# Attention products as pairs of 64-column tiles, one run per head, with new engine orders

## The chip, the cores and the metric

The kernel runs on one core of a Trainium2 chip, in one launch. The metric is the device time of that core in microseconds (us), the median of several runs. One execution was also recorded by the hardware profiler; its rows are what the working below rests on. Engine names are those of the profile: PE (TensorE, matrix products; PEld its weight loads), DVE (VectorE), ACT (ScalarE), POOL (GpSimd), SP (the queue that issues nearly all DMAs).

## The reference

Causal attention over 8 batches of 12 heads, 448 positions and 64 dimensions a head, followed by a soft mixture of experts on the result (3584 tokens of width 768, 8 experts of 4 slots):

```python
scores = scale * np.matmul(q, k.transpose(0, 1, 3, 2))
scores = np.where(mask, -1000000000.0, scores)          # mask: key behind query
scores = scores - np.max(scores, axis=-1, keepdims=True)
attn = np.exp(scores)
attn = attn / (np.sum(attn, axis=-1, keepdims=True) + 1e-09)
x = np.matmul(attn, v)                                  # then heads side by side: (3584, 768)

logits = x @ phi                                        # phi: (768, 32 slots)
slot_input = softmax_over_tokens(logits).T @ x
h = np.maximum(slot_input[e] @ w1[e], 0.0)              # per expert e, 4 slots each
slot_out[e] = h @ w2[e]
out = softmax_over_slots(logits) @ slot_out
```

All of it is float32 in and out.

## The kernel before

**Stages.** A short start (casts and the first scores), then a loop over the 96 heads (`for i in range(NHD)`), then the experts and the output. The loop works on pairs of heads (p = i // 2, h = i % 2), since q and k come in as pairs. While it runs, DMAs also bring the first 23 pieces of expert weights; the rest of the weights comes in after the loop.

**A head's way through the loop** is spread over several iterations. In iteration i:

- `scores1(i+2, ...)` on PE: the causal mask (parts c3, c0, c12, a product of `identb` and `tri`) and the first part of the scores (k0 to k3) go into a PSUM tile `s`, of which there are three. A head's scores are 4 blocks of 128 keys against the queries that may see them, 1024 columns in all.
- `max_keys(i+2, 0..3)` on DVE (x0 to x3): x0 is one TRANSPOSE_TENSOR_REDUCE of `s` (PSUM) into `r` (SBUF), x1 to x3 are three small TENSOR_TENSOR maxima of `r` with `r`, both inputs in SBUF.
- `max_row(i+1, 0)` (mr0): PE transposes `r` into the PSUM tile `rt`. `max_row(i+1, 1)` (mr1): DVE reduces `rt` to `mr`.
- `max_spread(i+1)` (sp): POOL spreads `mr` with an AFFINE_SELECT into rows of `r2` (the profile prints its name as `r`).
- `scores2(i, ...)` (t0 to t3) on PE: adds the rest of the scores and the spread maximum to `s`.
- `exps(i)` (exp): ACT writes exp(s) into `pt`, a tile in SBUF with one buffer for even and one for odd heads.
- `attv(i-1, ...)` (a0 to a3): PE multiplies blocks of `pt` with `va` (values and a column of ones, 65 columns) into the one PSUM tile `po`. Query block qc needs qc + 1 products, so 10 a head. Each is float32 and runs as two passes of one weight load and one matmul; the profile counts passes.
- `norm(i-1, 0..2)` (n0 to n2): DVE makes `sm` from `po` (a TENSOR_SCALAR and a RECIPROCAL) and writes `x` = `po` times `sm`.
- For the pair after next: `cast_k`, `cast_q` (ck, cq) and `copy_k2` (c2) on ACT; `sub_k` (sk, in even iterations) and `sub_q` (sq, in odd ones) on POOL, one TENSOR_TENSOR each, of two SBUF inputs.
- `plan`: in iterations fixed by number, one piece of the mixture: `xtrans` (4 transposes of `x` into `xt`, copied by ACT to `xts`), `next_logits` (8 products into `g` in tiles of 32 columns, then DVE adds into `lt`), `logits_e` (2 transposes into `tp`), `dispatch` (4 products into `sp` in tiles of 32 columns, then a DVE accumulation into `si`). `rt`, `xt`, `g`, `tp` and `sp` share one PSUM buffer (tag "m"), so the next one waits until the one before has been read.

**Order.** Nothing is reordered: every engine runs its instructions in the order in which the code emits them, and the framework adds the semaphore waits. Within an iteration that order is written out by hand, in the table `ORDER`, one row for even and one for odd iterations; an entry adds its instructions to the end of its own engine's queue. So the order on DVE is the order of the x, mr1 and n entries among each other, that on POOL the order of sp with sk or sq, and so on. "ld" runs a piece of the logits on ACT in one iteration of 12.

Of the kernel before, what the change touches and what calls it, by code (L numbers as in the profile page):

```python
# [17 lines left out]
P = 128  # L18
NB, NH, S, HD = 8, 12, 448, 64
NPAIR = NB * NH // 2  # L20
PPB = NH // 2
DM = NH * HD
NT = NB * S
NSLOT, NEXP, FF = 32, 8, 1024
# [6 lines left out]
NHD = 2 * NPAIR  # L31
# [13 lines left out]


ORDER = (
# [4 lines left out]
)  # L52

SC0, SC1, SC2, SC3 = 512, 0, 320, 960
# [30 lines left out]
def attention_soft_moe(ctx: ExitStack, tc: tile.TileContext, qk, va, phi, w1, w2, out):  # L85
    nc = _Core(tc)
# [36 lines left out]
    st = {}  # L123
# [199 lines left out]
        if i < NHD:  # L323
            nc.scalar.activation(out=pt_[i % 2][:, 0:1024], in_=st.pop(("s", i)), func=AF.Exp, scale=SCALE)

    def attv(i, qcs, first):
        if not 0 <= i < NHD:
            return
        p, h = divmod(i, 2)
        pt, v, po = pt_[i % 2], va_[p % 2], st.get(("po", i), po0)  # L330
        for qc in qcs:
            for c in range(qc + 1):
                col = SCOL[c] + P * (qc - c)


                m = P if qc < 3 or i == NHD - 1 and c < 3 else 65
                nc.tensor.matmul(po[0:m, qc], pt[:, col:col + m], v[:, c, h],
                                 start=c == 0 and qc in first, stop=c == qc, skip_group_check=True)

    def norm(i, k):  # L340
        if not 0 <= i < NHD:
# [20 lines left out]
    def xtrans(p):  # L362
        x = st.pop(("x", p))
        pt = misc(f"xt{p}")
        for c in range(NCH):
            nc.tensor.transpose(out=pt[:, P * c:P * c + P], in_=x[:, c], identity=ident)
        xt = st["xt", p] = xtp.tile([P, 512], F32, tag="xt", name=f"xts{p}", bufs=2)
        nc.scalar.activation(out=xt, in_=pt, func=AF.Copy)

    def logits_a(b, js, g, first=True, last=True):  # L370

        for j in js:
            xt = st.pop(("xt", b * PPB + j))
            for c in range(NCH):
# [14 lines left out]
    def logits_d(b, l):  # L389
        mo, mn = run_m[(b + 1) % 2], run_m[b % 2]  # L390
        al = st["al", b] = moe.tile([P, 1], F32, tag="al", name=f"al{b}", bufs=2)
        bs = st["bs", b] = moe.tile([P, 1], F32, tag="bs", name=f"bs{b}", bufs=2)
        nc.scalar.activation(out=gs, in_=l, func=AF.Exp, bias=mn[:, 0:1], accum_out=bs)
        nc.scalar.activation(out=al, in_=mo, func=AF.Exp, scale=-1.0, bias=mn[:, 0:1])
# [5 lines left out]
    def logits_e(b):  # L400
        tp = misc(f"tp{b}")
        nc.tensor.transpose(out=tp[:, 0:P], in_=gs, identity=ident)
        nc.tensor.transpose(out=tp[:, P:2 * P], in_=lt, identity=ident)
        st["dn", b] = gs.rearrange("p (c s) -> p c s", s=NSLOT)
        nc.scalar.activation(out=gs, in_=tp[:, 0:P], func=AF.Copy)
        nc.scalar.activation(out=lg[:, b], in_=tp[:, P:2 * P], func=AF.Copy)
        nc.scalar.activation(out=run_z, in_=run_z, func=AF.Identity, scale=st["al", b][:, 0:1],
                             bias=st.pop(("bs", b))[:, 0:1])
# [21 lines left out]
        dispatch_a(b, hf, sp)  # L430
        dispatch_b(b, hf, sp)

    plan = {}
    for b in range(NB):
        o, last = 12 * b, b == NB - 1
        for j, r in enumerate((3, 5, 9, 10, 12, 13)):
            if not last or j < PPB - 2:
                plan[o + r] = lambda p=b * PPB + j: xtrans(p)
        for j, r in ((0, 8), (2, 11)):
            plan[o + r] = lambda b=b, j=j: next_logits(b, j, misc(f"g{b}_{j}"))  # L440
        if not last:
            plan[o + 14] = lambda b=b: (next_logits(b, 4, misc(f"g{b}_4")), logits_b(b, lt))
            plan[o + 16] = lambda b=b: logits_e(b)
            plan[o + 18] = lambda b=b: dispatch(b, 0)
            plan[o + 19] = lambda b=b: dispatch(b, 1)

# [43 lines left out]
    run_z = const.tile([P, 1], F32, name="run_z")  # L490
    si = const.tile([P, DM], F32, tag="si", name="si")
    lg = const.tile([P, NB, NCH, NSLOT], F32, name="lg")
# [17 lines left out]
    for i in range(NHD):  # L510
        p, h = divmod(i, 2)
        if h:
            load_qk(p + 3, 1)
            if p + 1 < NPAIR - 1:
                loads_v(p + 1)
            load_qk(p + 3, 0)
            if p % 2 and nload < RES:
                load_w(nload)
                nload += 1
        if i == NHD - 3:  # L520

            loads_v(NPAIR - 1, nc.scalar)
        if i < 2:
            scores2(i, (1, 0, 2))
            if i:
                scores1_all(3)
            scores2(i, (3,))
            exps(i)
            if i == 0:
                max_row(1, 0)  # L530
                warm(START[4], po0.rearrange("p a b->p (a b)")[:, 0:P])
                max_row(1, 1)
                sub_k(1, h1, nc.vector)
                max_spread(1)
                sub_q(1, h1)

        qs = [int(n[1]) for n in ORDER[h] if n[0] == "a"]
        first = qs[:2] if qs[0] == 3 else qs[:1]
        for n in ORDER[h]:
            if i < 2 and (n == "exp" or n[0] in "kt" or n in ("c0", "c3", "c12")):  # L540
                continue
            if i == 0 and n in ("mr0", "mr1", "sp"):
                continue
            if n[0] == "k" or n in ("c0", "c3", "c12"):
                scores1(i + 2, n)
            elif n[0] == "t":
                scores2(i, (int(n[1]),))
            elif n[0] == "a":
                attv(i - 1, (int(n[1]),), first)
            elif n[0] == "x":  # L550
                max_keys(i + 2, int(n[1]))
            elif n[0] == "n":
                norm(i - 1, int(n[1]))
            elif n in ("mr0", "mr1"):
                max_row(i + 1, int(n[2]))
            elif n == "ld":
                if i % 12 == 3 and i > 12:
                    logits_d(i // 12 - 1, lt)
            elif n == "plan":
                if later and i:  # L560
                    later.pop(0)()
                plan.get(i, int)()
            else:
                {"exp": lambda: exps(i), "sp": lambda: max_spread(i + 1),
                 "ck": lambda: cast_k(p + 2), "sk": lambda: sub_k(p + 2), "cq": lambda: cast_q(p + 2),
                 "c2": lambda: copy_k2(p + 1), "sq": lambda: sub_q(p + 2)}[n]()
        if i == NHD - 1:

            scs.close()
            pe = att.enter_context(tc.tile_pool(name="pe", bufs=1, space=PSUM, reuse_waits="tile"))  # L570
            ps = [pe.tile([P, 512], F32, name=f"e{k}") for k in range(6)]

    i, b, p = NHD - 1, NB - 1, NPAIR - 1
# [8 lines left out]

    for k, qcs in ((2, (3, 2)), (4, (1, 0))):
        po = st["po", i] = ps[k][:, 0:NCH * VC].rearrange("p (c n) -> p c n", n=VC)
        attv(i, qcs, qcs[:1])
        cs = slice(qcs[1], qcs[0] + 1)
        nc.vector.tensor_scalar(out=sm[:, cs], in0=po[:, cs, HD], scalar1=EPS, scalar2=None, op0=ALU.add)
        nc.vector.reciprocal(out=sm[:, cs], in_=sm[:, cs])
        nc.vector.tensor_tensor(out=x[:, cs, HD:2 * HD], in0=po[:, cs, 0:HD],
                                in1=sm[:, cs].unsqueeze(2).to_broadcast([P, 2, HD]), op=ALU.mult)  # L590
# [17 lines left out]
    for c in range(NCH):  # L608
        nc.tensor.matmul(lp[32 * c:32 * c + 32, 0:P], phis[1][:, 2], xa[:, P * c:P * c + P],
                         start=False, stop=True, skip_group_check=True)  # L610
# [16 lines left out]
    for c in range(NCH):  # L627
        nc.tensor.matmul(tm[32 * c:32 * c + 32, P:P + 1], nm[:, 0:NSLOT], ident[:, 0:1],
                         start=True, stop=True, skip_group_check=True)
# [12 lines left out]
    for hf in range(2):  # L642
        tps = po0.rearrange("p a b->p (a b)")[:, 0:96] if hf == 0 else ps[2][:, 0:96]
        for c in range(3):
            o = 384 * hf + P * c
            nc.tensor.matmul(tps[:, NSLOT * c:NSLOT * c + NSLOT], si[:, o:o + P], sidw,
                             start=True, stop=True)
# [20 lines left out]

    hsb = const.tile([P, DM], F32, tag="si", name="hsb")

    def expert_in(e):
        hp = pt2.tile([P, 512], F32, tag="h", name=f"hp{e}")
        for dc in range(PPB):
            for f in range(4):
                k = 4 * dc + f
                w = wtiles[0, e, k // 12, k // 6 % 2][:, 256 * (k % 6):256 * (k % 6) + 256]
                nc.tensor.matmul(hp[32 * f:32 * f + 32, 0:256], slt[dc // 3][:, dc % 3], w,
                                 start=dc == 0, stop=dc == PPB - 1, skip_group_check=True)
        if e == 0:
# [119 lines left out]
    n = NBUF  # L799
# [42 lines left out]
def _layout(q, k, v, moe_phi, moe_w1, moe_w2):  # L842
# [9 lines left out]
    va = vp.reshape(NPAIR, 2, NCH, P, VC).transpose(0, 3, 2, 1, 4)  # L852
    phi = moe_phi.reshape(PPB, P, NSLOT).transpose(1, 0, 2)
    w1 = moe_w1.reshape(NEXP, PPB, P, 4, 256).transpose(0, 2, 1, 3, 4)
# [28 lines left out]
```

## Time and profile before

| what | value |
|---|---|
| median of 3 runs | 467.58 us (467.29 to 470.31) |
| the profiled execution: its own time | 467.8 us |
| its span, first to last instruction | 466.0 us, 1.8 us less than its time |
| mean granted TensorE clock | 0.985 |
| busy, of the span | PE 429.8, PEld 368.3, DVE 338.5, ACT 288.5, POOL 266.7 us |
| HBM read, written | 107.25 MB, 11.01 MB |

A row of the time view reads: start in us, duration in us, engine, line, operation, output <- inputs, shapes, count, and in brackets the idle time before it with what ended it. Several instructions of one kind in succession are merged into one row, whose duration is from the first start to the last end. All instructions of the kernel carry the line of the helper that records them, so groups are told apart by their tiles.

### The profile page before, as it was taken

The page shows a single profiled execution, that of the slowest core. Times are in us where ns is not written, and L with a number is a line of the kernel's source. Part 1 is how long each engine was busy: PE and PEld are TensorE (multiplying, and loading weights), DVE is VectorE, ACT ScalarE, POOL GpSimd, SP SyncE. Part 2 cuts the span into 40 slices and gives each one's busy share as a digit, 9 for nine tenths or more (in the row PEclk, how much of TensorE's full clock was granted, in tenths as well). Part 3 has the DMA queues.
Part 4 walks back from the last instruction along what each step waited for, and adds up shares of the span by engine and source line. Part 5 has one row for each costly group of instructions (what it writes and reads, how often), then busy time and mean ns, then how long its engine had stood idle before and what let it go on. Part 6 is the DMA issues. An engine that isn't in the chain of part 4 may idle for free.

```text
span 466.0 us, 11818 instructions
## 1 busy us (share of the span) xinstructions
PE 429.8 (92%) x4628; PEld 368.3 (79%) x4628; DVE 338.5 (73%) x954; ACT 288.5 (62%) x400; POOL 266.7 (57%) x216
## 2 busy tenths in 40 slices
PE   7799999999999999999999999999999999899850
PEld 3688998898999899988998899889988864454430
DVE  6888788878787888788788877887888447634350
ACT  5576777577767777777677677767774411243240
POOL 5788777776777677767776777677765100000000
PEclk9999999999999999999999999999999999999995
DMA  7376666765676656755676656765667999999998
GB/s 265 105 244 218 201 220 210 234 210 183 207 244 234 208 181 211 239 207 190 213 245 224 201 184 219 229 227 184 232 210 243 403 367 426 423 422 413 404 391 346
DMA packets 34471, 119.02 MB, mean 255 GB/s; under 512 B 3824, under 2 KB 8944, under 8 KB 32880
## 3 DMA queue, kind: packets, MB, share of 16 engines
q1 hardware_dynamic: 34272, 118.01, 71.8%
q8 instruction: 36, 0.59, 0.5%
q10 hardware_dynamic: 144, 0.27, 0.2%
q14 instruction: 19, 0.16, 0.1%
HBM read 107.25 MB, written 11.01 MB: 254 GB/s over the span
## 4 chain that ended last, share of the span: by engine, by line
PE 69%; DVE 14%; DMA 12%; issue 1%; ACT 1%; SPq 0%
PE po L69 31%; PE s L69 21%; DMA w<-in_w_dram 11%; DVE r L69 7%; PE xt L69 5%; PE sp L69 2%; DVE run_m L69 2%; PE g L69 2%; PE rt L69 2%; PE pp L69 1%; PE e L69 1%; DVE x L69 1%; DVE sm L69 1%; PE hp L69 1%; DMA qk<-in_qk_dram 1%
## 5 line engine op out<-in xcount | busy, mean ns | idle before, releaser
L69 PE MATMUL po<-va,pt 128*128 128x65 f32 x1900 | 193.3, 250 | 0.2 <-ACT xts L69 0.2
L69 PEld LDWEIGHTS po<-va,pt 128*128 128x128 f32 x1900 | 190.6, 170 | 0.5 <-ACT xts L69 0.4
L69 ACT ACTIVATE pt<-s 128x1024 f32<-128x1024 f32 x96 | 98.4, 1025 | 87.0 <-PE s L69 84.5
L69 DVE TRANSPOSE_TENSOR_REDUCE r<-s 128x32 f32<-128x1024 f32 x96 | 119.9, 1249 | 26.5 <-PE s L69 23.9
L69 POOL TENSOR_SCALAR_AFFINE_SELECT r<-mr 14x448 fp32r<-14x448 f32 x96 | 62.1, 646 | 86.9 <-DVE mr L69 60.4
L69 POOL TENSOR_TENSOR r<-qk,qd 64x896 fp32r<-64x896 f32 (+1 forms) x50 | 101.4, 2027 | 6.6 <-ACT qd L69 2.8
L69 POOL TENSOR_TENSOR ks<-qk,ks 64x896 fp32r<-64x896 f32 (+1 forms) x47 | 97.7, 2080 | 3.7
L69 PE MATMUL s<-r,k 128*128 128x320 f32 (+3 forms) x384 | 82.9, 297 | 2.2 <-POOL r L69 2.1
L69 PE MATMUL s<-qd,ks 128*128 128x448 f32 (+3 forms) x384 | 76.0, 308 | 0.9 <-ACT qd L69 0.8
L69 DVE TENSOR_TENSOR r<-r 128x10 f32<-128x10 f32 (+2 forms) x288 | 58.7, 204 | 9.8
L69 PEld LDWEIGHTS s<-r,k 128*128 128x128 f32 (+1 forms) x384 | 59.9, 176 | 5.8 <-POOL r L69 3.5
L69 PEld LDWEIGHTS s<-qd,ks 128*128 128x128 f32 (+1 forms) x384 | 55.1, 181 | 2.4 <-ACT qd L69 1.8
L69 ACT ACTIVATE ks<-qk 128x896 fp32r<-128x896 f32 (+1 forms) x50 | 45.7, 916 | 3.9 <-DMA qk<-in_qk_dram 2.7
L69 ACT ACTIVATE k<-ks 64x896 fp32r<-64x896 f32 (+1 forms) x49 | 45.8, 935 | 1.2
L69 ACT ACTIVATE qd<-qk 128x896 fp32r<-128x896 f32 (+1 forms) x50 | 45.7, 913 | 0.4 <-DMA qk<-in_qk_dram 0.3
L69 DVE TENSOR_TENSOR x<-po,sm 128x256 f32<-128x256 f32 x95 | 40.3, 425 | 3.3
L69 PEld LDWEIGHTS <-identb 128*128 128x128 bf16 x339 | 29.2, 99 | 16.5 <-issue 14.7
L69 PE MATMUL s<-tri,identb 128*128 128x64 bf16 (+2 forms) x288 | 39.8, 235 | 0.0
L69 PE MATMUL xt<-ident,x 128*128 128x128 f32 x188 | 29.9, 282 | 7.7 <-DVE mr L69 7.4
L69 ACT ACTIVATE xts<-xt 128x512 f32<-128x512 f32 x47 | 28.1, 597 | 11.5 <-PE xt L69 9.7
L69 DVE TENSOR_SCALAR sm<-po 128x4 f32<-128x4 f32 x95 | 15.1, 159 | 23.1 <-PE po L69 22.7
L69 DVE TENSOR_REDUCE mr<-rt 14x32 f32<-14x128 f32 x96 | 26.7, 278 | 2.5 <-PE rt L69 2.2
(135 smaller groups left out, 365.9 us busy)
## 6 DMA issues: line engine op xcount, KB each, us to landing
qk<-in_qk_dram SPq DMA_DIRECT2D x94, 448.0 KB, 3.3
w<-in_w_dram SPq DMA_DIRECT2D x43, 768.0 KB, 6.3
w<-in_w_dram SPq DMA_DIRECT2D x10, 1536.0 KB, 18.9
va<-in_va_dram SPq DMA_DIRECT2D x47, 260.0 KB, 3.4
out_dram<-ot SPq DMA_DIRECT2D x16, 384.0 KB, 6.7
out_dram<-ot SPq DMA_DIRECT2D x2, 1536.0 KB, 9.2
qk<-in_qk_dram SPq DMA_DIRECT2D x4, 224.0 KB, 3.4
hw<-in_w_dram SPq DMA_DIRECT2D x1, 768.0 KB, 6.3
```

The costliest lines, as they stand in the source:

```text
L69: return self._tc.keep_in_program_order(op(*args, **kwargs))
```

## The change

`attv` issues its products on 64 columns of `pt` at a time, instead of 128 (or 65 for the last query block): the output goes to partitions 0 to 63 or 64 to 127 of `po`, so that for query blocks 0 to 2 two products lie side by side in the array. The last query block (64 queries) is one product of 64 columns per key block. That is 16 products a head for 10. A set in `st` keeps which half of the tile has begun, for the start flag.

`ORDER` is rewritten. The 16 products of a head stand in one run at the end of an iteration, behind the scores, the transposed maximum and the transposes of `xtrans`; before, the products of query blocks 0 and 3 stood around the last part of the scores (t3), those of 1 and 2 behind it. `xtrans` and `logits_e`, whose matmuls are full width, move out of `plan` into an own table `plan_a`, called ahead of the run ("pa"); `next_logits` and `dispatch`, with their 32-column tiles, stay behind it. mr0, mr1 and sp now stand right behind the first part of the scores, ahead of t0 to t3 and of x0 to x3. On POOL the order stays sp, then sk or sq.

```diff
+AW = 64
 ORDER = (
-    ("c3", "c0", "k3", "c12", "k1", "k0", "k2", "t0", "t2", "t1", "a0", "a3", "t3", "ck",
-     "mr0", "exp", "x0", "a2", "x1", "x2", "x3", "mr1", "a1", "cq", "sp", "n0", "sk", "n1", "ld", "n2", "plan"),
-    ("c3", "c0", "k3", "c12", "k0", "k1", "k2", "t0", "t1", "t2", "a0", "x0", "t3", "a3", "exp", "mr0",
-     "x1", "x2", "x3", "mr1", "sp", "a2", "a1", "n0", "ld", "n1", "n2", "sq", "c2", "plan"),
+    ("ck", "c3", "c0", "k3", "c12", "k1", "k0", "k2", "mr0", "mr1", "sp", "sk", "t0", "t2", "t1", "t3", "exp", "pa",
+     "x0", "x1", "x2", "x3", "cq", "a0", "a1", "a2", "a3", "n0", "n1", "n2", "ld", "plan"),
+    ("c3", "c0", "k3", "c12", "k0", "k1", "k2", "mr0", "mr1", "sp", "t0", "t1", "t2", "t3", "sq", "exp", "c2", "pa",
+     "x0", "x1", "x2", "x3", "a0", "a1", "a2", "a3", "n0", "n1", "n2", "ld", "plan"),
 )
...
-    def attv(i, qcs, first):
+    def attv(i, qcs):
...
+        begun = st.setdefault(("begun", i, id(po)), set())
         for qc in qcs:
             for c in range(qc + 1):
                 col = SCOL[c] + P * (qc - c)
-                m = P if qc < 3 or i == NHD - 1 and c < 3 else 65
-                nc.tensor.matmul(po[0:m, qc], pt[:, col:col + m], v[:, c, h],
-                                 start=c == 0 and qc in first, stop=c == qc, skip_group_check=True)
+                for u in range(0, P if qc < 3 or i == NHD - 1 and c < 3 else 64, AW):
+                    nc.tensor.matmul(po[u:u + AW, qc], pt[:, col + u:col + u + AW], v[:, c, h],
+                                     start=u not in begun, stop=c == qc, skip_group_check=True)
+                    begun.add(u)
...
-    plan = {}
+    plan, plan_a = {}, {}
...
-                plan[o + r] = lambda p=b * PPB + j: xtrans(p)
+                plan_a[o + r] = lambda p=b * PPB + j: xtrans(p)
...
-            plan[o + 16] = lambda b=b: logits_e(b)
+            plan_a[o + 16] = lambda b=b: logits_e(b)
...
+            elif n == "pa":
+                plan_a.get(i, int)()
```

DVE's queue over one iteration, in the kernel before, in the middle of the loop: `s` and `r` are the scores and maxima of head i + 2, `rt` and `mr` those of head i + 1, `sm` and `x` the norm of head i - 1.

```order
L69 TENSOR_REDUCE r_2084<-s_2072 128x32
L69 TENSOR_TENSOR r_2084<-r_2084 128x10
L69 TENSOR_TENSOR r_2084<-r_2084 128x6
L69 TENSOR_TENSOR r_2084<-r_2084 128x2
L69 TENSOR_REDUCE mr_2097<-rt_2092 14x32
L69 TENSOR_SCALAR sm_2105<-po 128x4
L69 RECIPROCAL sm_2105<-sm_2105 128x4
L69 TENSOR_TENSOR x_100<-po,sm_2105 128x4x64
```

And DVE's queue in the changed kernel, over one iteration at the same head:

```order
L70 TENSOR_REDUCE mr_2298<-rt_2296 14x32
L70 TENSOR_REDUCE r_2315<-s_2288 128x32
L70 TENSOR_TENSOR r_2315<-r_2315 128x10
L70 TENSOR_TENSOR r_2315<-r_2315 128x6
L70 TENSOR_TENSOR r_2315<-r_2315 128x2
L70 TENSOR_SCALAR sm_2336<-po 128x4
L70 RECIPROCAL sm_2336<-sm_2336 128x4
L70 TENSOR_TENSOR x_100<-po,sm_2336 128x4x64
L70 TENSOR_REDUCE mr_2351<-rt_2349 14x32
```

Read as a circle, the eight instructions are the same, but `mr` has moved: before it stood between the three maxima and the norm, now it stands behind the norm and ahead of the next TRANSPOSE_TENSOR_REDUCE. POOL's rows beside it, in the changed kernel (in the kernel before they stand in the same order):

```order
L70 AFFINE_SELECT r_94<-mr_2298 14x448
L70 TENSOR_TENSOR r_91<-qk_20_2171,qd_85 64x896
L70 AFFINE_SELECT r_94<-mr_2351 14x448
L70 TENSOR_TENSOR ks_90<-qk_21_2283,ks_90 64x896
```

The spread of each `mr` is followed at once by one subtraction; nothing moved here, and each spread waits for the DVE row that writes its `mr`.

PE's queue from the transposed maximum to the next head's first scores, in the kernel before:

```order
L69 MATMUL s_1971<-r_91,k_93 128x448
L69 MATMUL s_1971<-r_91,k_93 128x320
L69 MATMUL s_1971<-r_91,k_93 128x192
L69 MATMUL po<-va_92,pt_95 128x65
L69 MATMUL s_1971<-r_91,k_93 64x64
L69 MATMUL po<-va_92,pt_95 65x65 x4
L69 MATMUL rt_2092<-ident,r_2041 14x128
L69 MATMUL po<-va_92,pt_95 128x65 x5
L69 MATMUL xt_2111<-ident,x_99 128x128 x4
```

And in the changed kernel:

```order
L70 MATMUL rt_2296<-ident,r_2257 14x128
L70 MATMUL s_2175<-r_91,k_93 128x448
L70 MATMUL s_2175<-r_91,k_93 128x320
L70 MATMUL s_2175<-r_91,k_93 128x192
L70 MATMUL s_2175<-r_91,k_93 64x64
L70 MATMUL xt_2308<-ident,x_99 128x128 x4
L70 MATMUL po<-va_92,pt_95 64x65 x16
```

The transposed maximum moved ahead of the second part of the scores, the products of `po` became one run of 16 behind everything else of the head, and the transposes of `x` stand ahead of that run instead of behind it.

More of the change, by code (lines that the diff above doesn't have):

```diff
@@ L535, in attention_soft_moe @@
                 sub_q(1, h1)
-        qs = [int(n[1]) for n in ORDER[h] if n[0] == "a"]
-        first = qs[:2] if qs[0] == 3 else qs[:1]
         for n in ORDER[h]:
@@ L548, in attention_soft_moe @@
             elif n[0] == "a":
-                attv(i - 1, (int(n[1]),), first)
+                attv(i - 1, (int(n[1]),))
             elif n[0] == "x":
@@ L584, in attention_soft_moe @@
         po = st["po", i] = ps[k][:, 0:NCH * VC].rearrange("p (c n) -> p c n", n=VC)
-        attv(i, qcs, qcs[:1])
+        attv(i, qcs)
         cs = slice(qcs[1], qcs[0] + 1)
```

## The prediction

> **What bounds the kernel now.** I first cut the span where the head loop ends, and read the busy time of each engine in the two stretches.
>
> ```profile
> core 0: us, PE busy (x) PEld busy (x) DVE busy (x) ACT busy (x) POOL busy (x), PEclk, DMA share, GB/s
> 18.06:363.80 345.74, 335.98 (x3628) 313.44 (x3629) 280.98 (x794) 248.80 (x315) 253.67 (x196) 1.00 0.65 213
> 364.00:466.00 102.00, 80.19 (x909) 46.23 (x907) 45.12 (x137) 28.13 (x69) 0.84 (x2) 0.93 1.00 401
> ```
>
> The second stretch, the experts, moves data with its DMA share at 1.00; the change touches nothing in it, and what it does to the loop only shifts it. In the loop PE is busy 97% of the time, DVE 81%, POOL 73%, DMA 65%, and the granted clock (PEclk) is full. So the loop decides. The length of a head comes from an instruction that runs once in 12 heads, in seven of the eight batches, with its first and last start:
>
> ```profile
> L69 DVE TENSOR_TENSOR run_m<-run_m,bm x7: 1284/1285/1303, 68.2 to 336.5; 128x1 f32<-128x1 f32 x7
> ```
>
> (336.5 - 68.2) / 72 heads = 3.73 us a head. Next I read what one head costs PE, from the chain of waits in order of time (start, us, engine and what):
>
> ```profile
> 194.52 1.14 PE s L69 x10
> 195.66 0.19 PE po L69 x2
> 195.85 0.03 PE s L69
> 195.88 0.50 PE po L69 x8
> 196.38 0.11 PE rt L69
> 196.49 1.06 PE po L69 x10
> 197.56 0.48 PE xt L69 x4
> ```
>
> The sum is 3.51 us, of which 1.75 are the 20 passes of `po`. Every head has one such extra as `xt` at the end. A reader who stops here would take all that is saved on `po` off the time. So I also read how DVE and POOL wait for each other (start, us, engine, operation):
>
> ```profile
> 208.96 0.28 DVE L69 TENSOR_REDUCE mr<-rt 14x32 f32<-14x128 f32 x1
> 209.31 0.64 POOL L69 TENSOR_SCALAR_AFFINE_SELECT r<-mr 14x448 fp32r<-14x448 f32 x1 [0.69 <-DVE mr L69]
> 209.49 0.16 DVE L69 TENSOR_SCALAR sm<-po 128x4 f32<-128x4 f32 x1 [0.25 <-PE po L69]
> 209.68 0.18 DVE L69 RECIPROCAL sm<-sm 128x4 f32<-128x4 f32 x1
> 209.90 0.42 DVE L69 TENSOR_TENSOR x<-po,sm 128x256 f32<-128x256 f32 x1
> 210.03 2.10 POOL L69 TENSOR_TENSOR ks<-qk,ks 64x896 fp32r<-64x896 f32 x1
> 210.46 1.25 DVE L69 TRANSPOSE_TENSOR_REDUCE r<-s 128x32 f32<-128x1024 f32 x1
> 211.74 0.81 DVE L69 TENSOR_TENSOR r<-r 128x10 f32<-128x10 f32 x3
> 212.47 0.28 DVE L69 TENSOR_REDUCE mr<-rt 14x32 f32<-14x128 f32 x1
> 212.82 0.64 POOL L69 TENSOR_SCALAR_AFFINE_SELECT r<-mr 14x448 fp32r<-14x448 f32 x1 [0.69 <-PE po L69]
> ```
>
> The reader is to see two things. POOL starts its subtraction (2.10 us) as soon as the spread is done. And the three maxima of `r` take 0.81 us here, from 211.74, though they come one right behind the other: the first is still running when the subtraction ends at 212.13. Such a **hold** is plainest where a DVE instruction of 128x1 with both inputs in SBUF meets a subtraction:
>
> ```profile
> 201.64 2.10 POOL L69 TENSOR_TENSOR ks<-qk,ks 64x896 fp32r<-64x896 f32 x1
> 202.47 1.28 DVE L69 TENSOR_TENSOR run_m<-run_m,bm 128x1 f32<-128x1 f32 x1
> ```
>
> One element a partition takes 1.28 us, and ends at 203.75, 0.01 behind POOL's 203.74. All seven of its kind do so (1284 to 1303 ns, quoted above). Instructions with PSUM among their inputs, and the reciprocal of one input, run beside POOL without such a stretch: RECIPROCAL and `x` above start and run in their usual times, the latter into the subtraction. From this comes a second limit, the circle mr, spread, subtraction, end of the held maximum, the other two, next mr: 208.96 to 212.47 is 3.51 us, as long as PE's path. The kernel has two limits of the same length; either alone keeps the time.
>
> **The change part by part.** *PE.* A pass of 65 columns costs 0.50 / 8 = 0.06 us. If two tiles side by side run at once, a head has 20 such steps (12 pairs and 8 single passes), 1.25 us; if they run one after another, 32, 2.0 us. That loads and products do run at once in column tiles is shown by the logits, four tiles of 32 columns side by side:
>
> ```profile
> 200.98 0.64 PE L69 MATMUL g<-xts,phi 128*32 128x128 f32 x16
> 201.56 0.26 PE L69 MATMUL s<-tri,identb 128*128 128x64 bf16 x2
> ```
>
> Sixteen passes of 128 columns are over in 0.58 us, where four full-width transposes of 128 columns take 0.48; so I take 1.25. On top comes what it costs to go into the tiles and out. Four steps at the transposes' 0.12 would be 0.48, so 0.1 of the 0.58 is the way out; I take as much again for the way in, 0.2 a head in all. PE's path is then 1.14 + 0.03 + 0.11 + 0.48 + 1.25 + 0.2 = 3.21 us, 0.30 less than now, and 3.96 if the pairs do not pair.
>
> The Trainium skill speaks against the change here: TensorEngine Tiling (Array Packing), section Key Properties, says that a change of tiling mode drains TensorE. By it each head pays two drains, which the 0.58 us above bears out; by a reading without it PE's path would be 3.01.
>
> *DVE and POOL.* Nothing is added, but `mr` now stands behind the norm (`sm`, reciprocal, `x`) and ahead of the TRANSPOSE_TENSOR_REDUCE. I walk one iteration with the durations above, clock at 0 where mr starts. mr ends at 0.28; spread 0.35 to 0.99; subtraction 1.07 to 3.17. On DVE the reduction starts 0.08 before mr ends (as mr itself does behind the maxima: 211.74 + 0.81 = 212.55 against 212.47), at 0.20; the first maximum follows a reduction's start by 1.28 (210.46 to 211.74), at 1.48. That is 0.41 behind the start of the subtraction and 1.69 ahead of its end: **it is held in every head until 3.20**. The other two end at 3.59, and the norm, which stood inside the subtraction's time before, now comes behind the hold: 209.49 to 210.32 is 0.83, less the overlap 0.08, so the next mr starts at 3.51 + 0.75 = 4.26. The circle has grown by the norm.
>
> Nothing else in the circle gives way: the subtraction cannot be late, for the cast that it needs stands early enough in the queue of ACT (72% busy in the loop): `cast_k` first of its iteration, `cast_q` an iteration ahead; the spread is ready 0.07 behind mr; the norm cannot pass the maxima in DVE's queue. PE's path of 3.21 lies inside 4.26 and so does 3.96, so the pairing no longer reaches the end, whichever it is: PE idles about 1 us a head, cover for its own mode changes and for `xt`, which waits for mr. That idling could lower the clock, which no row of the loop shows; in the experts' stretch, PE at 79%, the clock is still 0.93.
>
> *The pieces of the mixture.* `lt` and `si` run on DVE behind the norm, now in the circle, and the next `rt` waits in PE's queue until they have read the shared PSUM buffer. Their rows, that of `rt`, and two that show how soon PE starts what waited for DVE (205.72 to 205.77):
>
> ```profile
> L69 DVE SCALAR_TENSOR_TENSOR si<-si,al,sp 128x384 f32<-128x384 f32 x14 | 8.6, 614 | 0.6 <-PE sp L69 0.3
> L69 DVE TENSOR_TENSOR lt<-g,lt 128x128 f32<-128x128 f32 x13 | 3.6, 281 | 0.0
> L69 PE MATMUL rt<-ident,r 128*14 128x128 f32 x96 | 26.3, 274 | 2.2 <-DVE r L69 2.2
> ...
> 205.44 0.28 DVE L69 TENSOR_REDUCE mr<-rt 14x32 f32<-14x128 f32 x1
> 205.77 0.66 PE L69 MATMUL xt<-ident,x 128*128 128x128 f32 x4 [1.01 <-DVE mr L69]
> ```
>
> Behind either come `rt` (0.27) and two hand-overs of 0.05, 0.37, before the next mr: 0.65 for an `lt`, three in 12 heads (0.75 where two more small instructions follow), and 0.61 + 0.09 + 0.37 = 1.07 for an `si`, two in 12. Together 4.2 us per 12 heads; at least their bare time on DVE, 2.5. `logits_e` is read by ACT and costs the circle nothing. The start of the loop keeps its order, and SP's queue and the DMAs (0.65 of their time) only get more time. The casts on ACT keep their places within 4.26.
>
> **The sum.** The subtraction runs in 90 iterations (i from 2 to 91). Now: 90 x 3.73 = 335.4. Then: 90 x 4.26 + 7.5 x 4.2 = 383.4 + 31.5 = 414.9. The difference is +79.5; the last four heads, without a subtraction, and the last products give back about 2 (4 x 0.3 and 0.9). From the profiled 467.8 this gives 545.3; the median of the runs shown is 0.2 below that execution, so 545.
>
> **Rivals.** *Faster: the maximum is not held.* If it starts ahead of the subtraction, or that comes later, PE's path decides: 3.21 with `xt`, 3.27 with the mean extra of the 12 heads. A maximum that is not held takes about as long as the last of the three, which comes too late to be held, 0.16:
>
> ```profile
> L69 DVE TENSOR_TENSOR r<-r 128x10 f32<-128x10 f32 x80 | 16.9, 212 | 2.8
> ...
> L69 DVE TENSOR_TENSOR r<-r 128x2 f32<-128x2 f32 x80 | 12.9, 161 | 2.7
> ```
>
> The hold is then 3.20 - 1.48 - 0.16 = 1.56, and DVE alone needs 4.26 - 1.56 = 2.70, and 0.35 for the mixture, less than PE. 90 x (3.27 - 3.73) = -41, so 427. For it speaks that PE has 97% and the passes get cheaper; against it that it takes a shift of 0.41 us in a chain of three fixed durations. The point from which it decides is a subtraction that starts more than 1.48 behind mr's start.
>
> *Held in every other head.* If `sub_q`, whose cast stands in ACT's queue behind exp and `xts`, comes too late to hold, but `sub_k` does not, the time lies midway: (545 + 427) / 2 = 486. Against it: the cast is issued in the iteration before its subtraction.
>
> *The change does not pair.* With 32 passes one after another PE needs 3.96 and the circle still 4.26. What is left over, 0.3, is used up in heads with a longer extra:
>
> ```profile
> 216.47 0.78 PE sp L69 x8
> ```
>
> Against `xt`'s 0.48 that is 0.3 more, so next to nothing is added, 545 to 550. If then the hold fails too, PE alone gives 90 x (4.02 - 3.73) = +26, 494.
>
> **How the numbers follow.** The forecast gets 0.73, the faster rival 0.13, every other head 0.08, no pairing 0.04, and 0.02 are left for no change (1% is about what a measurement of this kernel can tell from none). The forecast's own ends: bare DVE time for the mixture, -13, and the circle 0.1 shorter, -9, give 523; 0.15 longer, +14, with waits on PE for each extra, +10, gives 569. The range takes in the case of every other head below, and leaves out the faster rival: 485 to 572. Faster 0.13, same 0.02, slower 0.85.
>
> **What would show it.** Right: `r<-r` 128x10 at about 1.7 us mean instead of 0.21, in nearly all heads; a head near 4.3 us with mr, spread and subtraction unchanged; PE busy under 80% in the loop, idle before `rt`, released by DVE `r`; `po` at 1.2 to 1.5 us a head. Wrong: `r<-r` short, PE still over 90% busy; or spreads that wait for something other than mr.

## The result: 548.2 us, slower by 17%, and the profile after

The changed kernel takes 548.2 us (median of 4 runs; 547.3 to 548.8), the kernel before 467.9 us (4 runs; 467.3 to 470.3). The ratio is 1.170, with a 95% interval from 1.166 to 1.175. The profiled execution spans 546.5 us, 80.5 more than before's 466.0.

From the page of the changed kernel: busy time, then three rows of the 40 slices.

```profile
PE 421.2 (77%) x5786; PEld 319.6 (58%) x5786; DVE 451.6 (83%) x954; ACT 288.3 (53%) x400; POOL 266.2 (49%) x216
...
PE   7676778778877877777778777776877699999870
...
DVE  5999999899989999999998999998999955753360
...
PEclk9999999898989899999998999999899999999995
```

DVE is now the full engine up to the end of the head loop, and it has 113 us more busy time (451.6 for 338.5), though its list of instructions is as long as it was. The loop alone, by the windows view (columns as in the prediction's first fence):

```profile
18.06:440.00 421.94, 325.82 (x4696) 263.96 (x4696) 391.18 (x787) 246.90 (x313) 253.04 (x196) 0.97 0.53 173
```

PE 77%, DVE 93%, POOL 60%, granted clock 0.97. The loop took 345.7 us up to 363.8 before and takes 421.9 up to 440.0 now. Where DVE's time went is seen in the groups by form (mean ns of one behind the busy time):

```profile
L70 DVE TENSOR_TENSOR r<-r 128x10 f32<-128x10 f32 x81 | 140.0, 1729 | 2.8
L70 DVE TENSOR_TENSOR r<-r 128x6 f32<-128x6 f32 x80 | 13.3, 166 | 2.8
L70 DVE TENSOR_TENSOR r<-r 128x2 f32<-128x2 f32 x80 | 12.9, 161 | 2.7
```

The first maximum takes 1729 ns on average, for 212 before. The other two, which come behind the subtraction, are short. One iteration of the circle in the timeline of DVE and POOL:

```profile
247.73 0.28 DVE L70 TENSOR_REDUCE mr<-rt 14x32 f32<-14x128 f32 x1
...
249.19 2.12 DVE L70 TENSOR_TENSOR r<-r 128x10 f32<-128x10 f32 x3
...
251.97 0.27 DVE L70 TENSOR_REDUCE mr<-rt 14x32 f32<-14x128 f32 x1
252.17 1.23 DVE L70 TRANSPOSE_TENSOR_REDUCE r<-s 128x32 f32<-128x1024 f32 x1
253.43 2.12 DVE L70 TENSOR_TENSOR r<-r 128x10 f32<-128x10 f32 x3
255.47 0.15 DVE L70 TENSOR_SCALAR sm<-po 128x4 f32<-128x4 f32 x1
```

```profile
252.32 0.64 POOL L70 TENSOR_SCALAR_AFFINE_SELECT r<-mr 14x448 fp32r<-14x448 f32 x1 [1.43 <-DVE mr L70]
253.04 2.10 POOL L70 TENSOR_TENSOR ks<-qk,ks 64x896 fp32r<-64x896 f32 x1
```

The maxima of the last head shown start at 253.43, 0.39 behind the subtraction; its end is at 255.14, and the three are over at 255.55. From mr to mr it is 251.97 - 247.73 = 4.24 us. The subtraction keeps its 2.10 us and starts 0.08 behind the end of the spread, as before. PE waits in the meantime (timeline of PE, idle time and its releaser in brackets):

```profile
247.34 0.28 PE L70 MATMUL rt<-ident,r 128*14 128x128 f32 x1 [1.66 <-DVE lt L70]
247.38 0.71 PE L70 MATMUL s<-r,k 128*128 128x448 f32 x4
248.06 0.66 PE L70 MATMUL xt<-ident,x 128*128 128x128 f32 x4
248.65 1.38 PE L70 MATMUL po<-va,pt 128*64 128x65 f32 x32
249.96 0.26 PE L70 MATMUL s<-tri,identb 128*128 128x64 bf16 x2
...
251.46 0.27 PE L70 MATMUL rt<-ident,r 128*14 128x128 f32 x1 [0.65 <-DVE sm L70]
```

A head's 32 passes of `po` go from 248.65 to 249.96, in 1.31 us; the pairs do run side by side. And PE then stands still ahead of `rt`, in both rows with an idle time released by DVE. The last row names `sm`, which does not feed `rt`. What does is the third maximum, and that ends at 249.19 + 2.12 = 251.31, 0.15 before `rt` starts at 251.46. In the next head it is 0.15 again (255.55 to 255.70).

### The profile page after: what moved, and what is told of

It reads as the page before. It is cut to its first block, busy times and chain, and to the rows that moved or that the text cites. A ratio compares the mean times of both kernels' runs of the same rounds, so it can differ in the third digit from the quotient of the medians.

```text
span 546.5 us, 14132 instructions
## 1 busy us (share of the span) xinstructions
PE 421.2 (77%) x5786; PEld 319.6 (58%) x5786; DVE 451.6 (83%) x954; ACT 288.3 (53%) x400; POOL 266.2 (49%) x216
## 5 line engine op out<-in xcount | busy, mean ns | idle before, releaser
L70 DVE TENSOR_TENSOR r<-r 128x10 f32<-128x10 f32 (+2 forms) x288 | 193.5, 672 | 9.8
L70 PE MATMUL po<-va,pt 128*64 128x65 f32 x3040 | 136.3, 230 | 0.3 <-issue 0.3
L70 PEld LDWEIGHTS po<-va,pt 128*64 128x64 f32 x3040 | 122.8, 142 | 14.1 <-issue 9.5
L70 DVE TRANSPOSE_TENSOR_REDUCE r<-s 128x32 f32<-128x1024 f32 x96 | 117.9, 1228 | 0.1
L70 PE MATMUL rt<-ident,r 128*14 128x128 f32 x96 | 26.5, 276 | 95.7 <-DVE lt L70 32.5
L70 PE MATMUL s<-qd,ks 128*128 128x448 f32 (+3 forms) x384 | 77.8, 313 | 2.2 <-ACT qd L70 2.2
L70 PEld LDWEIGHTS rt<-ident,r 128*14 128x14 f32 x96 | 8.4, 88 | 115.7 <-DVE lt L70 37.1
L70 PE MATMUL s<-r,k 128*128 128x320 f32 (+3 forms) x384 | 71.2, 307 | 0.5 <-POOL r L70 0.5
L70 PEld LDWEIGHTS s<-r,k 128*128 128x128 f32 (+1 forms) x384 | 55.4, 180 | 2.5 <-POOL r L70 0.7
L70 PEld LDWEIGHTS <-identb 128*128 128x128 bf16 x339 | 24.6, 99 | 20.5 <-issue 15.5
```

Source lines behind the costliest of these rows:

```text
L70: return self._tc.keep_in_program_order(op(*args, **kwargs))
```

## Experiments

The first question was which part costs the time: the pairs or the orders.

**The orders alone.** `ORDER` and `plan_a` of the changed kernel, products as before.

```diff
-                for u in range(0, P if qc < 3 or i == NHD - 1 and c < 3 else 64, AW):
-                    nc.tensor.matmul(po[u:u + AW, qc], pt[:, col + u:col + u + AW], v[:, c, h], ...)
+                m = P if qc < 3 or i == NHD - 1 and c < 3 else 65
+                nc.tensor.matmul(po[0:m, qc], pt[:, col:col + m], v[:, c, h], ...)
...
```

> The changed kernel's two orders, with the attention products of before: 128 (or 65) columns at a time, no pairs. Theory (the held maximum and the norm in the circle of DVE and POOL set the time): PE's path is 3.51 us a head and lies inside the circle's 4.24, so nothing is lost by giving up the pairs: 540 to 556 us, the 128x10 maximum at about 1.7 us mean. Rival (the tiles of 64 columns and their mode changes cost the time): the time falls back to that of before, 460 to 480 us, and the maximum stays short.

547.0 us, ratio to before 1.166 (1.158 to 1.173). In the groups by form the first maximum is as long as in the changed kernel:

```profile
L70 DVE TENSOR_TENSOR r<-r 128x10 f32<-128x10 f32 x81 | 139.5, 1722 | 2.8
```

The new orders alone bring the whole loss. With them the paired products gain nothing.

**The pairs alone.** The changed `attv` with before's `ORDER` and `plan` (the diff above in reverse, on the kernel before).

> The pairs of 64-column tiles alone, with the orders of before. Theory: the circle is back at 3.51 us a head, and PE saves about 0.55 us on the passes and pays 0.2 us for each of the two or three stretches of tiles into which that order cuts a head's products, so both limits stay near 3.5: 458 to 470 us. Rival (the tiles cost the time): 500 us or more. Rival (PE alone sets the time, and pairs bring what PE saves): 440 us or less.

471.6 us, ratio 1.006 (1.003 to 1.009): within 1% of before, and 1.6 us above the expected range. The chain of waits, an odd head (start, us, engine and what):

```profile
196.43 1.14 PE s L70 x10
197.57 0.27 PE po L70 x4
197.84 0.17 PE s L70
198.01 0.61 PE po L70 x8
198.62 0.21 PE rt L70
198.83 0.73 PE po L70 x20
199.56 0.59 PE xt L70 x4
```

The 32 passes of `po` take 0.27 + 0.61 + 0.73 = 1.61 us, for 1.75 before. But each full-width step next to them is longer than before: t3 0.17 for 0.03, `rt` 0.21 for 0.11, `xt` 0.59 for 0.48. These 0.35 are more than the 0.14 saved. In the even head ahead of it, whose products stand in two stretches and not in three, the same chain has 1.45 us of `po` for 1.70 before, and 0.27 more for t3 and `xt` (`rt` is as long as before there): no gain, and next to no loss. So with before's order the steps between the stretches of tiles eat the pairs' gain; that speaks for gathering the products into one run, as the change does.

**No subtraction on POOL.** The circle is cut at the suspected holder; the kernel leaves out a part of the scores.

```diff
-                 "sk": lambda: sub_k(p + 2),
+                 "sk": int,
...
-                 "sq": lambda: sub_q(p + 2)
+                 "sq": int
```

> The changed kernel without the subtractions of POOL in the loop (sub_k and sub_q from the third pair on are left out, so a part of the scores is left out; all else is the same). Theory: no maximum is held, the circle falls to about 2.7 us, and PE's path of 3.2 to 3.3 us a head sets the time: 425 to 440 us, the 128x10 maximum at 0.15 to 0.2 us. Rival (the order on PE, with one run of products behind everything, or the waits on the shared PSUM buffer set the time): 520 us or more.

437.7 us, ratio 0.933 (0.923 to 0.942). No maximum is held:

```profile
L70 DVE TENSOR_TENSOR r<-r 128x10 f32<-128x10 f32 x78 | 13.3, 171 | 2.7
```

This is 110 us from the changed kernel, with nothing taken from DVE or PE. It shows that the subtraction makes the loss, but not yet by which way, since POOL's own time is gone too. The next run keeps the subtraction.

**The subtraction behind the maxima.** A copy of one column of `r` on POOL (entry wx), which has to wait for the third maximum, stands ahead of the subtraction, and both stand behind x3.

```diff
-    ..., "mr0", "mr1", "sp", "sk", "t0", "t2", "t1", "t3", "exp", "pa", "x0", "x1", "x2", "x3", "cq", ...
+    ..., "mr0", "mr1", "sp", "t0", "t2", "t1", "t3", "exp", "pa", "x0", "x1", "x2", "x3", "wx", "sk", "cq", ...
-    ..., "t3", "sq", "exp", "c2", "pa", "x0", "x1", "x2", "x3", "a0", ...
+    ..., "t3", "exp", "c2", "pa", "x0", "x1", "x2", "x3", "wx", "sq", "a0", ...
+            elif n == "wx":
+                nc.gpsimd.tensor_copy(out=scr, in_=st["r", i + 2][:, <last column of x3>])
```

> The changed kernel with each subtraction of POOL issued behind a copy of one column of r, which waits for the last of the three maxima: the subtraction then starts behind the maxima instead of under them, and runs beside the norm, mr and the reduction. Everything is computed. Theory: no maximum is held, the subtraction (2.1 us) ends before the next head's maxima, and PE's path of 3.2 to 3.3 us sets the time: 425 to 445 us. Rival (any order with mr ahead of the maxima is slow, since POOL's own time, 3.0 us with the copy, or the waits for spreads become the limit): 460 to 520 us.

457.1 us, ratio 0.974 (0.966 to 0.981). The mechanism is confirmed, since the same work in the same order on DVE and PE, and a copy more on POOL, takes 91 us less than in the changed kernel; but the expected 425 to 445 was too fast. The groups by form show what is left:

```profile
L70 DVE TENSOR_TENSOR r<-r 128x10 f32<-128x10 f32 x78 | 21.7, 278 | 2.7
L70 DVE TENSOR_TENSOR r<-r 128x6 f32<-128x6 f32 x78 | 21.4, 274 | 2.7
...
L70 DVE TENSOR_TENSOR run_m<-run_m,bm 128x1 f32<-128x1 f32 x7 | 8.5, 1208 | 0.2
```

`run_m`, with two inputs in SBUF, is now held seven times by the moved subtraction, for 1.2 us each. And the maxima are still longer than 170 ns on average, because of the other POOL instruction (timeline):

```profile
202.49 0.92 DVE L70 TENSOR_TENSOR r<-r 128x10 f32<-128x10 f32 x3
...
202.56 0.64 POOL L70 TENSOR_SCALAR_AFFINE_SELECT r<-mr 14x448 fp32r<-14x448 f32 x1
```

The three take 0.92 us here, for some 0.5 unheld (171 + 166 + 161 ns above). The spread, which runs from 202.56 to 203.20, holds too, but with 0.64 us for at most that long. Besides, a head with `xt` needs 3.46 us on PE, for the prediction's 3.21 (timeline of PE, with ACT's copy):

```profile
203.79 0.27 PE L70 MATMUL rt<-ident,r 128*14 128x128 f32 x1
...
206.60 0.60 ACT L70 ACTIVATE xts<-xt 128x512 f32<-128x512 f32 x1
207.25 0.28 PE L70 MATMUL rt<-ident,r 128*14 128x128 f32 x1
```

From `rt` to `rt` it is 207.25 - 203.79, and the second starts 0.05 behind the end of the copy of `xt`, out of the buffer that the two share.

**run_m with one SBUF tensor.** The same, with `bm` given as a scalar per partition, and the copy cut to one partition.

```diff
-        nc.vector.tensor_tensor(out=mn, in0=mo, in1=st.pop(("bm", b)), op=ALU.min)
+        nc.vector.tensor_scalar(out=mn, in0=mo, scalar1=st.pop(("bm", b))[:, 0:1], scalar2=None, op0=ALU.min)
...
-                nc.gpsimd.tensor_copy(out=scr, in_=st["r", i + 2][:, <last column of x3>])
+                nc.gpsimd.tensor_copy(out=scr, in_=st["r", i + 2][0:1, <last column of x3>])
```

> The kernel with the late subtraction (457 us), with two edits: the small min of run_m and bm as a TENSOR_SCALAR with bm as its per-partition scalar, so one tensor input instead of two, and the waiting copy on POOL on one partition. Everything is computed. Theory: seven holds of 1.2 us go, of which a large part is on the path: 448 to 454 us. Rival (an operand given as a scalar is held like a tensor): 455 to 458 us.

451.5 us, ratio 0.964 (0.961 to 0.967), 5.6 us less. Its `run_m` is not held any more (min, median and max in ns, in the list by tile):

```profile
L70 DVE TENSOR_SCALAR run_m<-run_m,bm x7: 213/214/215, 65.9 to 321.5; 128x1 f32<-128x1 f32 x7
```

The first of the seven starts at 65.86, inside a subtraction of POOL (64.95 to 67.03), and takes its 0.21 us all the same. 7 x (1208 - 214) ns are 7.0 us, for 5.6 gained. What the smaller copy brings of these was not run apart; it takes 0.17 us for 0.18.

**The transposes' copy ahead of copy_k2.** On top of that, ACT's copy of `xt` moves ahead of `copy_k2` in odd iterations, so that the shared buffer is free earlier.

```diff
-    ..., "exp", "c2", "pa", "x0", ...
+    ..., "exp", "pa", "c2", "x0", ...
```

> As the kernel with the two edits, and in odd iterations ACT copies xt ahead of copy_k2 instead of behind it, so that the shared PSUM buffer is free sooner for the next transposed maximum. Theory (PE waits 0.1 to 0.2 us for that copy in some 20 heads): 2 to 4 us less than without it. Rival (copy_k2 then comes late for the second part of the scores): the same or more.

447.3 us, ratio 0.955 (0.952 to 0.959), 4.2 us less, a little more than the 2 to 4 expected. This version beats both kernels. Its loop, by the windows view:

```profile
18.00:341.00 323.00, 310.15 (x4700) 258.24 (x4701) 286.41 (x789) 245.90 (x314) 269.86 (x289) 1.00 0.70 226
```

PE is at 96%, for 97% in the kernel before, and the clock at 1.00.

**The same with products of 128 columns.** The best version with before's products (the diff of the first experiment).

> The kernel with the late subtraction and all three edits (447 us), with the attention products of before, 128 (or 65) columns at a time. Theory: with the hold gone PE's path sets the time, so now the pairs are worth what they save on PE: 1.75 us a head for 1.31 and 0.15 to 0.25 of mode changes, 0.2 to 0.3 us, over 92 heads: 465 to 476 us. Rival (PE is not the limit even there): 446 to 450 us.

470.0 us, ratio 1.002 (0.999 to 1.006), in the expected range. So the pairs are worth 470.0 - 447.3 = 22.7 us once the circle is out of the way, and the circle out of the way is worth nothing without the pairs.

```profile
18.00:364.00 346.00, 343.95 (x3606) 314.63 (x3606) 271.88 (x790) 247.92 (x316) 270.41 (x289) 1.00 0.67 212
```

PE is at 99% of its loop.

**A shorter norm.** In the changed kernel, n2 writes 8 columns of 64 in heads 18 to 89, so a DVE step that is in the circle, but runs without POOL, is cut.

```diff
+            nd = HD if i < 18 or i >= 90 else 8
-            nc.vector.tensor_tensor(out=st["x", p][:, :, HD * h:HD * h + HD], ...
+            nc.vector.tensor_tensor(out=st["x", p][:, :, HD * h:HD * h + nd], ...
```

> The changed kernel, in which the last instruction of the norm writes only 8 of 64 columns of x for heads 18 to 89 (the rest of x is left out there), so it takes about 0.2 us instead of 0.42. Theory (the norm stands in the circle): each of 72 heads is shorter by 0.2 to 0.25 us, 14 to 18 us in all: 528 to 536 us. Rival (DVE is only held by POOL, and the norm fits in between): 546 to 549 us.

534.6 us, ratio 1.141 (1.137 to 1.147), 13.6 less than the changed kernel, within the expected range.

```profile
L70 DVE TENSOR_TENSOR x<-po,sm 128x32 f32<-128x32 f32 x72 | 13.8, 191 | 2.5
```

The cut is 424 - 191 = 233 ns in 72 heads, 16.8 us at most. The norm does lie in the circle. In heads without an extra on DVE only 0.13 of it comes through (from mr to mr 4.11 us for 4.24): there mr starts 0.38 behind the start of `rt`, as it does in the heads with `lt`, where the profile names `rt` as what it waits for. In heads with an extra 0.21 to 0.23 comes through.

**Longer between spread and subtraction.** A copy of constants on POOL stands between the two, 128, 384 or 640 columns wide, in three kernels.

```diff
+            elif n == "wx":                      # ORDER: "sp", "wx", "sk" and "t3", "wx", "sq"
+                if i < NHD - 4:
+                    nc.gpsimd.tensor_copy(out=scr, in_=ident)      # or ident 3 or 5 times, by broadcast
```

The copy of 128 columns:

> The changed kernel with one more instruction on POOL in each head, a copy of a constant 128x128 tile between the spread and the subtraction (such a copy took 0.32 us in the kernel before). Nothing on DVE, PE or ACT reads it. Theory (spread, subtraction, end of the held maximum, norm and mr are one circle): each head is longer by the copy and its start, 0.40 us, over 90 heads 36 us: 578 to 590 us. Rival (POOL is idle for 1.4 us a head, so it has room): 548 to 552 us.

559.0 us, ratio 1.193 (1.188 to 1.199). The direction is right, the size was not. The copy takes 0.28 us and starts 0.05 ahead of the spread's end, and from the start of the spread to that of the subtraction it is 0.96 us for 0.72 in the changed kernel, so a head grows by 0.24 us, not by 0.40. Besides, the first heads of the loop are faster: mr starts at 16.25 and, seven heads on, at 39.38, 3.3 us a head. In the changed kernel the same seven heads go from 19.32 to 48.98, 4.24 us each, so 6.5 us are won there, which the expectation did not have. Two rows of POOL from the middle and one from that start:

```profile
252.79 0.64 POOL L70 TENSOR_SCALAR_AFFINE_SELECT r<-mr 14x448 fp32r<-14x448 f32 x1 [1.42 <-DVE mr L70]
253.38 0.28 POOL L70 COPY scr<-ident 128x128 f32<-128x128 f32 x1
...
28.01 0.64 POOL L70 TENSOR_SCALAR_AFFINE_SELECT r<-mr 14x448 fp32r<-14x448 f32 x1
```

The row at 28.01 has no idle time before it: POOL is behind there, and its subtraction comes at another place of DVE's round. This suggested a second, lasting way: if the subtraction comes late enough, the maximum is over before it. The copies of 384 and 640 columns were to reach it:

> The changed kernel with a copy of 384 columns on POOL between spread and subtraction, instead of the 128 columns of the run before (0.28 us there; about 0.65 us expected here). In that run the first 9 heads, in which POOL also had its memsets and no idle time, took 2.9 to 3.9 us, and all later ones 4.5 or more. Theory with two ways of running: as long as POOL has more to do per head than PE it never catches up with mr, spreads come a head's maxima late, and the subtraction does not begin just ahead of the maxima; with 3.6 to 3.7 us of work on POOL a head this lasts to the end, and the kernel gets faster by more work: 455 to 485 us. Rival (one circle alone, in which POOL's work adds): 0.6 us a head longer than the changed kernel, 595 to 610 us.

562.3 us, ratio 1.196 (1.185 to 1.207): between the two expected ranges, so both theories missed. The groups by form say why:

```profile
L70 DVE TENSOR_TENSOR r<-r 128x6 f32<-128x6 f32 x76 | 149.7, 1970 | 2.6
L70 POOL COPY scr<-ident 128x384 f32<-128x384 f32 x76 | 37.5, 493 | 0.0
L70 DVE TENSOR_TENSOR r<-r 128x10 f32<-128x10 f32 x76 | 13.0, 171 | 2.6
```

The first maximum does slip through, in 171 ns. The second is held in its place.

> As the run with the copy of 384 columns (which took 0.49 us, less than estimated, so that POOL's work, 3.35 us a head, stayed below PE's 3.45), with 640 columns, about 0.7 us, so 3.57 us of POOL work a head. Two ways of running: POOL now has more to do than PE, stays late for every mr, and most heads take 3.6 to 3.9 us: 455 to 490 us. One circle alone: the subtraction begins about 1.75 us behind mr's start, behind the first two maxima (1.48 and 1.69) and ahead of the third (1.89), which is held to 3.87, then the norm: 4.5 us a head, 558 to 570 us.

567.8 us, ratio 1.209 (1.189 to 1.229), in the range expected of one circle alone (558 to 570). Now it is the third:

```profile
L70 DVE TENSOR_TENSOR r<-r 128x2 f32<-128x2 f32 x75 | 145.6, 1942 | 2.6
L70 POOL COPY scr<-ident 128x640 f32<-128x640 f32 x76 | 53.8, 708 | 0.0
```

In all three the circle has about the same length, 4.5 us: one maximum of the three always meets the subtraction, and all that follows waits for it. What a longer delay adds is won back by the maxima that are over before the hold. A delay that lets all three pass was not run, so the lasting fast way stays open for mere delays; that a subtraction behind the third maximum is fast is shown above.

## Why the prediction was right, point by point

- **Two limits of one length before.** Borne out from PE's side: with the circle out of the way and old products, the time stays (1.002), with PE at 99%. That the circle alone would keep it was not tried on its own, since the pairs with before's order did not shorten PE's path; so this half is argued only.
- **The hold in every head.** "Held in every head until 3.20": 81 maxima of 1729 ns mean, the longest 1745, so none was short: the rival of every other head is out. An iteration takes 4.24 us for the forecast's 4.26. Without the subtraction, or with it behind the maxima, the hold goes, and with it 110 and 91 us.
- **The norm in the circle.** The shorter norm shows it, 13.6 of at most 16.8 us.
- **PE's path does not reach the end.** The orders alone give 547.0, the whole change 548.2. Of the path's terms, one run of pairs and the way in and out of the tiles were put at 1.25 + 0.2; measured are 1.31, with the way out in it, and 0.59 for the `xt` ahead of it (248.06 to 248.65) instead of 0.48, in all 1.42. The rival that the change does not pair is out too. The Trainium skill's drain at a change of tiling mode (TensorEngine Tiling (Array Packing), Key Properties) agrees with the trace: in the kernel with the pairs alone the full-width steps beside stretches of tiles are longer by 0.10 to 0.14 us.
- **The pieces of the mixture.** The instruction that runs once in 12 heads gives the sum with the extras:

```profile
L70 DVE TENSOR_TENSOR run_m<-run_m,bm x7: 158/158/158, 80.8 to 414.1; 128x1 f32<-128x1 f32 x7
```

(414.1 - 80.8) / 6 = 55.55 us for 12 heads, where the prediction has 12 x 4.26 + 4.2 = 55.3. Heads with `lt` take 4.96 (0.72 extra for 0.65), those with `si` 5.29 (1.05 for 1.07). These terms alone, 12 x 4.24 + 3 x 0.72 + 2 x 1.05, would give 55.1: the head was put a little too long and the `lt` too short, and it is luck that the two nearly cancel. What is above 55.1 is for the most part the clock (next point). The 0.23 more in 12 heads make 1.7 of the 3 us by which 545 fell short; the rest is not traced.
- **The clock.** "That idling could lower the clock": the loop's mean is 0.97, but it is not low throughout. The granted clock is 1.00 in most heads (from 187.6 to 289.0 and from 298.8 to 382.0, for example) and falls to about 0.6 for some 4 to 5 us in a few (windows view, the stretch behind `rt` of one such head, and the next head):

```profile
178.10:182.20 4.10, 4.09 (x42) 3.62 (x42) 3.48 (x5) 2.35 (x3) 2.73 (x2) 0.58 0.28 100
183.00:187.00 4.00, 3.35 (x49) 2.75 (x48) 3.73 (x8) 3.29 (x4) 2.74 (x2) 1.00 0.56 181
```

```profile
180.24 2.03 PE L70 MATMUL po<-va,pt 128*64 128x65 f32 x32
182.30 0.16 DVE L70 TENSOR_SCALAR sm<-po 128x4 f32<-128x4 f32 x1 [0.23 <-PE po L70]
```

There the products take 2.03 us for 1.38, DVE waits for them ahead of the norm, and from mr to mr it is 4.78 us for 4.24. Two more such heads (mr at 127.47 and 294.56) take 4.84. Together that is 1.7 us, so the lowered clock does reach the end, though by little; in two other heads with a clock of 0.64 and 0.67 PE's idle time covers it. In each of these three heads PE had stood idle for 1.7 us ahead of `rt`, behind an `lt`; but so it had at 247.34 above (1.66), and no fall came. That the idling is what lowers the clock is not shown. With the orders alone, where PE is busy 86% of its loop, the clock is 1.00 and 12 heads take (409.9 - 78.9) / 6 = 55.2 us.

Of the signs, one came out otherwise than named: the long waits of `rt` are put down to `lt`, `si` and `sm`, not to `r`. For `lt` and `si` that is the wait for the shared PSUM buffer, which the prediction had; for `sm`, the starts 0.15 behind the end of the maxima (above) speak for `r` all the same.

Three things were wrong in the working. The faster rival was priced too low: 427 by a PE path of 3.27, where the run without the subtraction gives 437.7 and, by its `run_m`, 41.4 / 12 = 3.45 us a head. What it lacks is the waits for the shared PSUM buffer: `rt` waits for ACT's copy of `xt`, and for the `si` and `lt` of DVE (waits view of that run: what waits, for what, us, times, longest).

```profile
PEld rt L70 <- ACT xts L70: 8.5, 31, 1.0
PEld rt L70 <- DVE si L70: 4.6, 14, 0.4
PEld rt L70 <- DVE lt L70: 3.1, 14, 0.3
```

They come to 16.2 us, and the missing 0.18 in 90 heads to as much. That each of these waits is lost at the end is argued only; moving the copy of `xt` forward brought 4.2 us. The experiment with the subtraction behind the maxima was put too low in part by the same step, in part by the held `run_m` and the holds of the spread. Then, only the subtraction was counted as a holder. In the changed kernel that is enough, since the spread is over before the maxima; where the subtraction stands behind them, the spread holds them too. And the point "more than 1.48 behind mr's start" is right for the first maximum only: with the copy of 384 columns the subtraction starts 1.53 behind mr, and the second is held. All three must have begun, some 0.4 later: the third starts behind the first two, of 171 and 166 ns, and the short gaps after them. With the copy of 640 columns the subtraction starts 1.74 behind mr, and the third is held.

## What to carry to other kernels

Before adding up what a cheaper product saves on the full engine, look for loops between the engines that are not full: here a DVE instruction with two SBUF inputs that fell under a POOL instruction on SBUF lasted to that one's end, and the order that put both into one dependent circle made this circle the bound. When an order is written by hand, put the long POOL instruction where DVE has work from PSUM or with one SBUF tensor, and pin it there with a dependence; POOL's own order, the same in both kernels, did not. Gather tiled products into one run, and test a change of order and a change of products apart: here one lost 79 us, the other is worth 23, and only once the subtraction stands behind the maxima.

## What the runs showed of the hardware that was not expected

- The AFFINE_SELECT on POOL, 14x448 in 0.64 us, holds DVE's maxima as the subtraction does: three maxima of some 0.5 us took 0.92. The Trainium skill (SBUF — State Buffer, SBUF: two separate sides) says that a DVE instruction with two SBUF inputs and a POOL instruction that reads SBUF lock each other out for a whole instruction; the traces agree for both POOL instructions, in the one direction that they show, DVE held by POOL.
- The same minimum of 128x1 takes 1208 ns (held) as an instruction of two tensors and 214 ns with the second input as a scalar per partition, at the same place of the order, under a running subtraction both times.
- A step at full width beside products in 64-column tiles is longer by 0.10 to 0.14 us (`rt`, `xt`, t3 in the odd head with the pairs alone; in the even head `rt` is not).
- A mean granted clock of 0.97 can hide short falls: in the changed kernel's loop it is 1.00 in most heads and 0.58 to 0.67 for 4 to 5 us in a few.
